# Another queue for one value chunk, and shorter fillers, in the prologue of a fused attention and feed-forward kernel

## The chip, the cores and the metric

The kernel runs on one core of a Trainium2 chip. A core has a matrix engine (TensorE, PE in the profile), a vector engine (VectorE, DVE), an activation engine (ScalarE, ACT), a general engine (GpSimd, POOL) and an engine that only issues transfers (SyncE, SP). Sixteen DMA engines carry all transfers, whichever engine issues them. Each engine runs its own instructions in their order, and semaphores order them against each other. The metric is the device time of one execution in microseconds; smaller is better.

## The reference

An attention layer with two parts is followed by a feed-forward layer. `q`, `k` and `v` are 8 batches x 8 heads x 576 positions x 64 numbers.

```python
q_d, k_d, v_d = (t.reshape(B, H, 144, 4, D).mean(axis=3) for t in (q, k, v))
out_up = np.repeat(softmax(scale * q_d @ k_d.T) @ v_d, 4, axis=2)
mask = np.abs(pos[:, None] - pos[None, :]) < 4          # a band of 7 keys per query
out_local = softmax(np.where(mask, scale * q @ k.T, -1e9)) @ v
x = (out_up + out_local).transpose(0, 2, 1, 3).reshape(4608, 512)
h = x @ w_in                                             # 512 -> 2048
out = (h * sigmoid(1.702 * h)) @ w_out                   # 2048 -> 512
```

All inputs and the output are fp32; the kernel multiplies in bf16.

## The kernel before

The 4608 rows of `x` fall into 9 groups of 512 for the feed-forward part, and the attention goes batch by batch (576 rows). The loop over groups `g` runs the two products of group `g` (`mm1`, L682, and `mm2`, L746) and puts batch `g + 1`'s attention in slots between their matmuls. The order on every engine is the order of the program text; nothing is planned or rearranged. The change edits the prologue alone, L789 to L878, which computes batch 0's attention by itself and starts group 0's first product.

**Value chunks.** The 576 keys of a batch are held as five overlapping chunks of 2 x 64 keys. Chunk `i` of `vb` has one half on partitions 0 to 63 and one on 64 to 127, each filled by a transfer of its own. `load_vb` (L219) issues the two transfers on POOL, which reads fp32 from memory and writes bf16 to `vb`. `load_v` (L203) issues on SyncE and writes fp32 to a tile `vf`; a cast (`prep_v`, L305) then makes `vb` of it. Before the change, batches 0 and 1 use `load_vb`; `load_v` is first used for batch 2. If `load_v` is given a `gate`, an engine writes one element of `vf` first, and the transfers on SyncE wait for that write, as they overwrite it.

**POOL's order at the start** is: four transfers of `kb` and `qb` (with `iota` instructions among them), ten of `vb` (two for each chunk), the first quarter of `w_in` (`load_w_in(0, 512)`), two additions for `qdT` (`pool_qk`, L297 and L301), the other three quarters of `w_in`, the next batch's `kb` and `qb`, and half of `w_out`. An issue on POOL waits for the landing of the transfer that POOL issued eight before it.

**TensorE's order in the prologue** is: fillers (`warm`, L637, products of the zero tiles `wz`, bf16, or `wf`, fp32, which nobody reads); local scores of the first four heads (L355, L367); fillers; local scores of the other four (which wait for `qT`, L267); downsampled scores (L379); a filler; the downsampled values from chunks 0 and 1 (`prep_vd_pe`, L336, `kc` = 0); fillers; those from chunks 1, 2 and 3 (`kc` = 1); local attention times values for two head pairs (`av_local0`, L511, chunks 0 to 4 in order); the downsampled values from chunks 3 and 4 (`kc` = 2); scores (L379); the downsampled attention (`av_down0`, L525 and L534); the third head pair; a filler (L863); the turned sums (`transp_sum`, L576 and L587); the fourth pair; and from 24.00 us on the first feed-forward matmuls (L682), first on `w_in`'s first quarter.

**ScalarE's order** there: the selection matrices `psel` (L173 to L178), `exp_local` for the first four heads and for the other four (L417, writes `es`), `exp_down` (L423, writes `ed`), and the copies of `prep_vd_pe` (L345, writes `vd`).

Of the kernel before, what the change touches and what calls it, by code (L numbers as in the profile page):

```python
# [19 lines left out]
def kernel(  # L20
# [9 lines left out]
    nc = tc.nc  # L30
# [38 lines left out]
    PM = [psum.tile([128, 512], FP32, name=f"pm{i}") for i in range(2)]  # L69
# [8 lines left out]
    def pm_tile():  # L78
        turn["m"] += 1
        return PM[turn["m"] % 2]  # L80

    wz = consts.tile([128, 512], BF16, name="wz")
    wf = consts.tile([128, 512], FP32, name="wf")
    off = consts.tile([128, 60], BF16, name="off")
    psel = consts.tile([128, 7, 64], BF16, name="psel")
# [27 lines left out]
    def fill():  # L113
        nc.vector.memset(wz, 0.0)
        nc.vector.memset(wf, 0.0)
        for t in kdT:
            nc.vector.memset(t[:, SD:160, :], 0.0)
        for t in vbs:
            nc.vector.memset(t[:, :, :, 64:65], 1.0)
        for t in vds:  # L120
            nc.vector.memset(t[:, :, :, 64:65], 4.0)
        for t in es:
            nc.vector.memset(t[:, :, 300:304], 1.0)
        for t in eds:
            nc.vector.memset(t[:, :, 432:480], 1.0)


    def make_off():
        nc.vector.tensor_tensor(out=dm, in0=dm, in1=dm, op=ALU.mult)
        nc.vector.tensor_single_scalar(out=dm, in_=dm, scalar=9.5, op=ALU.is_lt)  # L130
        nc.vector.tensor_scalar(
            out=off, in0=dm, scalar1=-1.0, scalar2=1e6, op0=ALU.add, op1=ALU.mult
        )
# [13 lines left out]
    def make_bias():  # L147
        nc.vector.memset(bias[:, 3:4], -3.0)
        nc.vector.tensor_copy(out=bias[:, 0:2], in_=rv)
        nc.vector.tensor_scalar(  # L150
            out=bias[:, 0:2], in0=bias[:, 0:2], scalar1=-1.0, scalar2=400.0,
            op0=ALU.add, op1=ALU.mult,
        )
# [17 lines left out]
    def end_psel():  # L171
        for m in range(7):
            nc.scalar.activation(  # L173
                out=dp[:, m], in_=di[:, 0:64], func=AF.Abs, scale=8.0, bias=db[:, m : m + 1]
            )
        nc.scalar.activation(out=dp, in_=dp, func=AF.Relu, bias=bias[:, 3:4])
        for sl, c in ((slice(0, 1), 1), (slice(1, 7), 0)):
            nc.scalar.activation(  # L178
                out=psel[:, sl], in_=dp[:, sl],
                func=AF.Exp, scale=-400.0, bias=bias[:, c : c + 1],  # L180
            )
# [21 lines left out]
    def load_v(b, gate=None, chunks=range(5)):  # L203
        t = ldp.tile([128, 5, H, D], FP32, name="vf", tag="vf")
        vf[b] = t
        if gate is not None:
            gate(t[0:1, 0, 0, 0:1])
        for i in chunks:
            for par in range(2):
                nc.sync.dma_start(  # L210
                    out=t[64 * par : 64 * par + 64, i],
                    in_=bass.AP(
                        tensor=v.tensor,
                        offset=v[b, 0].offset + (114 * i + KSTART[par]) * D,
                        ap=[[D, 64], [S * D, H], [1, D]],
                    ),
                )

    def load_vb(b, i):  # L219
        for par in range(2):  # L220
            nc.gpsimd.dma_start(  # L221
                out=vbs[b % 2][64 * par : 64 * par + 64, i, :, 0:D],
                in_=bass.AP(
                    tensor=v.tensor,
                    offset=v[b, 0].offset + (114 * i + KSTART[par]) * D,
                    ap=[[D, 64], [S * D, H], [1, D]],
                ),
            )
# [34 lines left out]
    def prep_1(name, b, qd):  # L263
        store, dst = {"k": (kf, kT), "q": (qf, qT)}[name]
        tt = work.tile([128, S, 2], BF16, name=f"{name}T{qd}", tag=f"{name}T{qd}", bufs=1)
        t32 = tt.rearrange("p t a -> p (t a)").bitcast(FP32)
        nc.vector.transpose(  # L267
            out=t32.rearrange("p (i c) -> p c i", c=18),
            in_=store[b, qd].bitcast(FP32).rearrange("p (c d) -> p c d", c=18),
        )  # L270
        dst[b, qd] = tt
# [33 lines left out]
    def prep_v(b, eng, i=slice(0, 5), h=slice(0, H)):  # L305
        cp = eng.copy if eng is nc.scalar else eng.tensor_copy
        cp(out=vbs[b % 2][:, i, h, 0:D], in_=vf[b][:, i, h])  # L307
# [17 lines left out]
    def prep_vd_pe(b, pv, kcs=range(3), between=None):  # L325
        hp0, n = 0, HP
        vb, vd = vbs[b % 2], vds[b % 2]
        for kc, iis in ((0, (0, 1)), (1, (1, 2, 3)), (2, (3, 4))):
            if kc not in kcs:
                continue  # L330
            c0 = 256 * (kc - kcs[0])
            if between and kc == 1:
                between()
            for i in iis:
                for j in range(2):
                    nc.tensor.matmul(  # L336
                        pv[64 * j : 64 * j + 64, c0 : c0 + D * n],
                        lhsT=psel[:, PSEL.index((i, kc)), :],
                        rhs=vb[:, i, :, :].rearrange(
                            "p (hp j) d -> p hp j d", j=2  # L340
                        )[:, hp0 : hp0 + n, j, 0:D],
                        start=(i == iis[0]), stop=(i == iis[-1]),
                        tile_position=(0, 64 * j),
                    )
        nc.scalar.copy(  # L345
            out=vd[:, kcs[0] : kcs[-1] + 1, :, 0:D],
            in_=pv[:, 0 : 256 * len(kcs)].rearrange(
                "p (k h d) -> p k h d", k=len(kcs), h=HP
            ),
        )  # L350
# [26 lines left out]
    def score_d(b, qd, sd, kc, a, r):  # L377
        rows, j = slice(32 * r, 32 * r + 32), r % 2
        nc.tensor.matmul(  # L379
            sd[64 * j : 64 * j + 64, r // 2, SD * kc : SD * kc + SD],  # L380
            lhsT=kdT[qd][rows, 48 * kc : 48 * kc + 64, a],
            rhs=qdT[b, qd][rows, :, a],
            start=(a == 0), stop=(a == 1),
            tile_position=(32 * r, 64 * j),
        )

    def scores(b, qd, sp):
        bar_others(sp)
        for i in range(5):
            for a in range(2):  # L390
                for par in range(2):
                    for r in range(4):
                        score(b, qd, sp, i, a, par, r, barred=True)
        return sp

    def scores_d(b, qd, sd):
        for kc in range(3):
            for a in range(2):
                for r in range(4):
                    score_d(b, qd, sd, kc, a, r)  # L400
        return sd
# [13 lines left out]
    def exp_local(qd, sp):  # L415
        for u in range(2):
            nc.scalar.activation(  # L417
                out=es[2 * qd + u][:, :, 0:300], in_=sp[u][:, :, 0:300],
                func=AF.Exp, scale=inv_sqrt_d,
            )  # L420

    def exp_down(qd, sd):
        nc.scalar.activation(  # L423
            out=eds[qd][:, :, 0:432], in_=sd[:, :, 0:432],
            func=AF.Exp, scale=inv_sqrt_d / 16.0,
        )
# [115 lines left out]
    def y_tiles0():  # L542
        return (
            work.tile([128, 2, 6, D], BF16, name="yl", tag="yl", bufs=4),
            work.tile([128, 2, 2, D], BF16, name="yd", tag="yd", bufs=4),
            work.tile([128, 2, 7, 1], FP32, name="rc0", tag="rc0", bufs=4),
        )
# [89 lines left out]
    def warm(n, cols=512, t=None, z=wz):  # L637
        t = pm_tile() if t is None else t
        for _ in range(n):
            nc.tensor.matmul(  # L640
                t[:, 0:cols], lhsT=z[:, 0:128], rhs=z[:, 0:cols], start=True, stop=True
            )
# [150 lines left out]
    load_1("q", q, qf, 0, 1)  # L793
    iota_psel()
    fill()
    for i in range(5):
        load_vb(0, i)
    load_w_in(0, 512)
    warm(3, z=wf)
    warm(2)  # L800
    make_off()
    make_ident(di)
    make_psel()
    make_bias()
    end_psel()
    prep_1("k", 0, 0)
    prep_1("q", 0, 0)
    sp = scores(0, 0, PA[0:2])
# [13 lines left out]
    warm(2, z=wf)  # L822
    sp = scores(0, 1, PA[0:2])
    exp_local(1, sp)
    exp_down(0, scores_d(0, 0, PA[2]))
    for hp in range(4):
        o[hp] = PA[hp % 3]
        y[hp] = y_tiles0()
    warm(1, z=wf)
    prep_vd_pe(0, PM[0], range(0, 2), lambda: warm(2, t=PM[1]))  # L830
    for hp in range(2):
        av_local0(hp, o[hp], range(5))
        normalise0(o[hp], y[hp], hp % 2, "a")
# [18 lines left out]
    def av_whole0(hp):  # L852
        av_local0(hp, o[hp], range(5))
        av_down0(hp, o[hp])
        normalise0(o[hp], y[hp], hp % 2)
# [4 lines left out]
        copy_x(0, hp, PM if n is None else PA[n][:, :, 0:288])  # L860

    av_whole0(2)
    warm(1, t=PM[0], z=wf)  # L863
    turned(0, None)
    av_whole0(3)
    turned(1, 1)
# [90 lines left out]
```

## Time and profile before

| what | value |
|---|---|
| median of three runs | 316.63 us (315.98 to 320.5) |
| profiled execution: time, span of the instructions | 317.56 us, 315.8 us |
| TensorE busy | 307.7 us, 97% of the span |
| first feed-forward matmul (L682) starts | 24.00 us |
| idle time of TensorE just before 16.66 us, 22.56 us, 24.89 us | 0.24, 1.11, 0.29 us |
| granted TensorE clock, mean | 0.998 |
| landing of chunks 3 and 4 of `vb`, second halves | 15.69 us, 16.62 us |
| landing of the first quarter of `w_in` | 20.7 us |

Times within the kernel count from the span's start. A line of a timeline gives start and duration in microseconds, the engine, the line of the kernel, the operation, what it writes and reads, shape and type, and how many; in brackets stands the idle time of the engine before it and what ended it, where "issue" means that the engine waited for nothing that the profile shows. A line of the view by windows gives the stretch, its length, then for TensorE's matmuls, its weight loads, VectorE, ScalarE and GpSimd the busy time with the number of instructions started, and then the granted clock, the DMA share and GB/s. In the DMA view q0 is POOL's queue, q1 SyncE's, and q8 carries instructions; a line gives packets, MB and the time that the packets took as a share of 16 engines. A landing is the time from issue until the last of a transfer has arrived.

### The profile page before, as it was taken

The page shows a single profiled execution, that of the slowest core. Times are in us where ns is not written, and L with a number is a line of the kernel's source. Part 1 is how long each engine was busy: PE and PEld are TensorE (multiplying, and loading weights), DVE is VectorE, ACT ScalarE, POOL GpSimd, SP SyncE. Part 2 cuts the span into 40 slices and gives each one's busy share as a digit, 9 for nine tenths or more (in the row PEclk, how much of TensorE's full clock was granted, in tenths as well). Part 3 has the DMA queues.
Part 4 walks back from the last instruction along what each step waited for, and adds up shares of the span by engine and source line. Part 5 has one row for each costly group of instructions (what it writes and reads, how often), then busy time and mean ns, then how long its engine had stood idle before and what let it go on. Part 6 is the DMA issues. An engine that isn't in the chain of part 4 may idle for free.

```text
span 315.8 us, 10270 instructions
## 1 busy us (share of the span) xinstructions
PE 307.7 (97%) x4543; PEld 154.3 (49%) x4543; DVE 123.5 (39%) x247; ACT 190.2 (60%) x348; POOL 138.8 (44%) x170
## 2 busy tenths in 40 slices
PE   7989999999999999999999999999999999999995
PEld 3455455445544455455544554455445544444444
DVE  6763824720673057604760377027801640000000
ACT  5445882767657685668566856584767576316611
POOL 8863782179339920794079505960393000000000
PEclk9999999999999999999999999999999999999999
DMA  7999999999959913995299519971920110020011
GB/s 119 122 187 210 187 86 205 190 196 261 181 162 224 202 47 98 188 204 113 87 203 206 112 56 206 208 136 39 173 46 11 58 71 2 15 85 33 2 66 66
DMA packets 64075, 39.97 MB, mean 127 GB/s; under 512 B 44064, under 2 KB 55456, under 8 KB 64032
## 3 DMA queue, kind: packets, MB, share of 16 engines
q1 hardware_dynamic: 44496, 24.32, 36.0%
q0 software_dynamic: 19392, 14.95, 33.5%
q8 instruction: 35, 0.57, 0.8%
q14 instruction: 8, 0.07, 0.1%
q10 hardware_dynamic: 144, 0.07, 0.1%
HBM read 44.83 MB, written 9.44 MB: 172 GB/s over the span
## 4 chain that ended last, share of the span: by engine, by line
PE 91%; DMA 4%; ACT 1%; POOL 1%; issue 1%; DVE 0%; POOLq 0%; DVEq 0%; ACTq 0%
PE pm L746 36%; PE pm L682 35%; PE pa L682 4%; PE pa L367 2%; PE pa L439 2%; DMA qb<-in_q_dram 2%; PE pa L490 2%; PE pa L379 2%; PE pa L746 2%; PE pa L448 2%; DMA vb<-in_v_dram 1%; PE pm L761 1%; ACT od L610 1%; PE pm L640 0%; POOL vb L221 0%
## 5 line engine op out<-in xcount | busy, mean ns | idle before, releaser
L746 PE MATMUL pm<-w_out_bf,gT 128*128 128x512 bf16 x528 | 120.3, 380 | 0.0
L682 PE MATMUL pm<-xT,w_in_bf 128*128 128x512 bf16 x512 | 119.2, 379 | 0.5 <-ACT xT L603 0.3
L693 ACT ACTIVATE gT<-pm 128x512 bf16<-128x512 f32 x128 | 76.3, 598 | 43.7 <-PE pm L682 43.7
L682 PEld LDWEIGHTS <-w_in_bf 128*128 128x128 bf16 x576 | 55.7, 98 | 66.9 <-issue 1.1
L746 PEld LDWEIGHTS <-gT 128*128 128x128 bf16 x560 | 52.3, 98 | 60.7 <-issue 0.5
L431 DVE TENSOR_TENSOR es<-es,mask 128x600 bf16<-128x600 bf16 x28 | 19.0, 694 | 97.0 <-ACT es L417 96.3
L297 POOL TENSOR_TENSOR pq<-kT 128x576 f32<-128x576 bf16 x13 | 15.1, 1165 | 60.8 <-DVE kT L267 60.8
L731 ACT ACTIVATE osb<-pm 128x512 f32<-128x512 f32 (+2 forms) x35 | 20.4, 587 | 25.8 <-PE pm L746 23.0
L476 DVE TENSOR_TENSOR y<-pa,rc 128x896 bf16<-128x896 f32 x28 | 30.6, 1092 | 1.0
L480 ACT COPY y<-y 64x64 bf16<-64x64 bf16 x28 | 6.7, 241 | 31.3 <-DVE y L476 31.3
L417 ACT ACTIVATE es<-pa 128x600 bf16<-128x600 f32 x32 | 19.7, 668 | 8.7 <-PE pa L367 8.6
L313 POOL TENSOR_TENSOR v<-v 112x512 f32<-112x512 f32 x18 | 23.0, 1279 | 0.0
L307 POOL CAST vb<-vf 128x2560 bf16<-128x2560 f32 x6 | 13.9, 2318 | 19.8 <-DMA out_dram<-osb 6.3
L267 DVE STREAM_TRANSPOSE kT<-kb 128x576 f32<-128x576 f32 x16 | 19.9, 1246 | 5.8 <-DMA kb<-in_k_dram 5.6
L733 DVE TENSOR_SCALAR osb<-pm 128x128 f32<-128x128 f32 x1 | 0.3, 292 | 55.2 <-ACT osb L731 55.2
L632 DVE TENSOR_TENSOR xT<-pa,od 128x456 bf16<-128x456 bf16 (+2 forms) x84 | 16.6, 255 | 12.3 <-ACT od L610 12.1
L267 DVE STREAM_TRANSPOSE qT<-qb 128x576 f32<-128x576 f32 x16 | 19.9, 1243 | 0.8 <-DMA qb<-in_q_dram 0.4
L682 PE MATMUL pa<-xT,w_in_bf 128*128 128x512 bf16 x64 | 20.0, 379 | 0.0
L610 ACT COPY od<-pa 128x256 bf16<-128x256 bf16 (+1 forms) x56 | 18.3, 410 | 1.1 <-PE pa L490 0.4
L367 PEld LDWEIGHTS <-kT 32*64 32x64 bf16 x1280 | 14.2, 104 | 6.9 <-issue 4.1
L221 POOL DMA_DIRECT2D vb<-in_v_dram x20 | 13.7, 703 | 8.6 <-DMA w_in_bf<-in_moe_w_in_dram 3.6
L367 PE MATMUL pa<-qT,kT 32*64 32x60 bf16 x1280 | 16.5, 198 | 0.5 <-DVE qT L267 0.5
(90 smaller groups left out, 275.9 us busy)
## 6 DMA issues: line engine op xcount, KB each, us to landing
out_dram<-osb SPq DMA_DIRECT2D x35, 256.0 KB, 2.4
vf<-in_v_dram SPq DMA_DIRECT2D x60, 128.0 KB, 6.8
v<-in_v_dram SPq DMA_DIRECT2D x36, 192.0 KB, 5.4
kb<-in_k_dram POOLq DMA_DIRECT2D x16, 288.0 KB, 7.7
qb<-in_q_dram POOLq DMA_DIRECT2D x16, 288.0 KB, 8.9
w_in_bf<-in_moe_w_in_dram POOLq DMA_DIRECT2D x4, 512.0 KB, 9.2
w_out_bf<-in_moe_w_out_dram POOLq DMA_DIRECT2D x4, 512.0 KB, 12.5
vb<-in_v_dram POOLq DMA_DIRECT2D x20, 64.0 KB, 5.9
```

The source lines that it names most:

```text
L267: nc.vector.transpose(out=t32.rearrange("p (i c) -> p c i", c=18), in_=store[b, qd].bitcast(FP32).rearrange("p (c d) -> p c d", c=18),)
L313: eng.tensor_tensor(out=t1[0:112], in0=x[:, :, 0:2, :], in1=x[:, :, 2:4, :], op=ALU.add)
L367: nc.tensor.matmul(sp[r // 2][64 * par : 64 * par + 64, r % 2, 60 * i : 60 * i + 60], lhsT=kT[b, qd][rows, k0 : k0 + 64, a], rhs=qT[b, qd] ...
L417: nc.scalar.activation(out=es[2 * qd + u][:, :, 0:300], in_=sp[u][:, :, 0:300], func=AF.Exp, scale=inv_sqrt_d,)
L431: nc.vector.tensor_tensor(out=ev, in0=ev, in1=mask, op=ALU.mult)
L476: nc.vector.tensor_tensor(out=y.rearrange("p (x c) d -> p x c d", x=2), in0=ov[:, :, :, 0:D], in1=rc.to_broadcast([128, 2, 7, D]), op=ALU. ...
L610: nc.scalar.copy(out=od[:, 4 * t0 : 4 * (t0 + n)].rearrange("p (t f) -> p t f", f=4), in_=x[:, xx, c0 : c0 + n, None].to_broadcast([128, n ...
L632: nc.vector.tensor_tensor(out=sub(xT[hp], t0 + at, *dims), in0=sub(x, col, *from_x), in1=sub(od, at, *dims), op=ALU.add,)
L682: nc.tensor.matmul(acc, lhsT=w_in_bf[:, dmc, ffc * 128 : (ffc + 1) * 128], rhs=xT[dmc][:, g * TG : g * TG + TG], start=(dmc == 0), stop=(d ...
L693: nc.scalar.activation(out=gT[:, ffc, :], in_=acc, func=AF.Silu, scale=GELU_SCALE)
L731: eng.activation(out=osb, in_=ap, func=AF.Copy, scale=1.0 / GELU_SCALE)
L746: nc.tensor.matmul(ops[t], lhsT=gT[:, ffc, t * 128 : (t + 1) * 128], rhs=w_out_bf[:, ffc, :], start=(ffc == 0), stop=(ffc == n_ffc - 1),)
```

## The change

Chunk 4 of batch 0's values is no longer loaded by POOL (`range(4)` for `range(5)`). Instead `load_v` loads it as fp32 on SyncE's queue into `vf`, behind a gate: ScalarE copies one element of `psel` into the chunk, just after it has made `psel`. The gate's element now lies in the first chunk that is loaded, which is the same place as before for the other uses. ScalarE casts the chunk to `vb` between `exp_local(1, ...)` and `exp_down(0, ...)`. `w_in` and everything behind it on POOL are issued two transfers sooner. Four places of fillers on TensorE are changed: 2 x 512 columns to 2 x 256 (first scores); one fp32 product of 512 columns to two bf16 of 128 (before chunk 0's use); 2 x 512 to 2 x 256 (between `kc` = 0 and 1); and one fp32 product of 512 to two bf16 of 512 (before the turned sums).

```diff
@@ load_v
         if gate is not None:
-            gate(t[0:1, 0, 0, 0:1])
+            gate(t[0:1, chunks[0], 0, 0:1])
@@ prologue
     fill()
-    for i in range(5):
+    for i in range(4):
         load_vb(0, i)
     load_w_in(0, 512)
     warm(3, z=wf)
-    warm(2)
+    warm(2, 256)
     make_off()
     make_ident(di)
     make_psel()
     make_bias()
     end_psel()
+    load_v(0, lambda t: nc.scalar.copy(out=t, in_=psel[0:1, 6, 0:1]), [4])
     prep_1("k", 0, 0)
...
     sp = scores(0, 1, PA[0:2])
     exp_local(1, sp)
+    prep_v(0, nc.scalar, 4)
     exp_down(0, scores_d(0, 0, PA[2]))
...
-    warm(1, z=wf)
-    prep_vd_pe(0, PM[0], range(0, 2), lambda: warm(2, t=PM[1]))
+    warm(2, 128)
+    prep_vd_pe(0, PM[0], range(0, 2), lambda: warm(2, 256, t=PM[1]))
...
     av_whole0(2)
-    warm(1, t=PM[0], z=wf)
+    warm(2, t=PM[0])
     turned(0, None)
```

## The prediction

> **What bounds the kernel now.** I read the page's first two parts, then TensorE's timeline of the first 25 us, then the DMA view. TensorE is the bound: busy 97% of the span, and from 24.00 us on it stands still for hardly a microsecond before the tail. The change edits only the prologue, so what it is worth is by how much it moves the first matmuls of the dense part (L682, 24.00 us).
>
> ```profile
> PE 307.7 (97%) x4543; PEld 154.3 (49%) x4543; DVE 123.5 (39%) x247; ACT 190.2 (60%) x348; POOL 138.8 (44%) x170
> ...
> q8 instruction: 35, 0.57, 0.8%
> ```
>
> TensorE's timeline (start, duration, engine, line):
>
> ```profile
> 13.68 1.12 PE L640 MATMUL pm<-wf 128*128 128x512 f32 x2
> 14.74 0.42 PE L336 MATMUL pm<-vb,psel 128*64 128x256 bf16 x4
> 15.09 0.60 PE L640 MATMUL pm<-wz 128*128 128x512 bf16 x2
> 15.62 0.53 PE L336 MATMUL pm<-vb,psel 128*64 128x256 bf16 x6
> 16.09 0.34 PE L511 MATMUL pa<-vb,es 64*64 64x65 bf16 x17
> 16.66 0.41 PE L511 MATMUL pa<-vb,es 64*64 64x65 bf16 x23 [0.24 <-DMA vb<-in_v_dram]
> ...
> 19.94 1.12 PE L640 MATMUL pm<-wf 128*128 128x512 f32 x2
> ...
> 22.56 0.33 PE L587 MATMUL pm<-id,yl 128*128 128x57 bf16 x5 [1.11 <-issue]
> ```
>
> Two waits stand there. The 0.24 us at 16.66 is the one that the change removes: chunk 4 lands at 16.62. The other, 1.11 us at 22.56, waits for no engine and no data ("issue"). It comes from instruction loading. 35 packets of 16 KB on q8 for 9086 matmuls and weight loads are one per 260 instructions (63 bytes each), so I take blocks of 256 of 64 bytes. The view by windows counts what had started before the wait at 22.56, before the one other "issue" wait in the attention (53.57) and before 16.13:
>
> ```profile
> 0.00:16.13 16.13, 13.62 (x222) 6.44 (x225) 11.35 (x32) 7.84 (x16) 13.49 (x30) 1.00 1.38 121
> 0.00:21.60 21.60, 18.64 (x351) 9.52 (x351) 15.77 (x45) 10.97 (x20) 18.14 (x37) 1.00 1.33 137
> 0.00:53.50 53.50, 49.05 (x862) 25.46 (x863) 29.86 (x62) 30.65 (x53) 35.86 (x60) 1.00 1.32 158
> ```
>
> TensorE stands after 702 and after 1725 instructions: 1023 apart, four blocks. So a block ends at 702, and the one before it at about 447, reached at 16.13 in the first L511 matmuls. I read it so: passing 447 asks for the block that begins at 703. The DMA view narrowed to 20.0 to 20.5 us holds that block's packet:
>
> ```profile
> q8 instruction: 1, 0.02, 11.2%
> ```
>
> It starts at 20.11, takes 0.9, and TensorE goes on at 22.55: **6.42 us from the request to use**. This is the chain that sets 22.55; the 1.06 us filler at 20.01 lies inside it. What decides is when L511 begins, and before it L336 needs chunk 3. The second half of chunk 3 is issued at 10.99 and lands 4.7 later, at 15.69:
>
> ```profile
> DMA to landing us min/median/max: 4.7/4.7/4.7
> ```
>
> The L336 matmuls on chunk 3 start at 15.77, 0.08 later. **Chunk 3, not chunk 4, sets the request.**
>
> **The change part by part.** *Fillers.* The first wz pair (0.84 at 7.01) falls to half: 0.2 us at most, since L367 waits for qT (8.06); the next scores wait for qT at 12.04 anyway. Then 1.06 us of fp32 becomes two of 128 columns (0.1), and 0.43 becomes 0.22: TensorE would reach chunk 3's matmuls 1.2 us sooner and now waits there for the landing instead. The last fp32 filler becomes two bf16 ones, 1.06 to 0.43: 0.63 less, ahead of the block wait. Each filler keeps its number of matmuls and loads (the fp32 one is recorded as two of each), so block ends stay at the same instructions.
>
> *POOL.* Two issues of 0.69 go, so w_in's first piece is issued at 11.7, not 12.99, qdT's sums end at 14.4, not 15.76 (used at 17.36), and the pieces behind follow 1.4 sooner. Worth nothing: w_in's first piece lands at 20.7 and is first used at 24.00.
>
> *ScalarE.* The gate copy (0 to 0.24, the 64x64 copy of L480) follows psel at 8.29, in an idle stretch until 9.19. The cast is taken as 0.59 (L345's cast of 128x512), behind es at 14.15. It waits for the landing: SyncE's queue is empty until 52.71, its two issues go out at about 8.5 and 9.2, and vf transfers land after 6.8 us (median of 60), so 16.0; the bounds are 1.6 (the quickest store), so no wait, and 17. Behind the cast stand exp_down (0.90) and vd's copy; with 16.0 the first ends at 17.5 and the second finds its matmuls done at about 17. av_down0 (17.99 now) asks for them at about 19. Cover: 1.5 us here, and 1.7 us in the block wait (below). Nothing on the path.
>
> *The DMA engines.* Here is the cost. Chunk 4's 1024 packets leave the end of POOL's queue, where they delayed nobody but themselves, and go out on SyncE's queue while chunks 0 to 3 are in flight. Packets by queue in 10:11, 99:100, 102:103 and 76:78 us:
>
> ```profile
> q0 software_dynamic: 1206, 0.15, 248.8%
> ```
> ```profile
> q1 hardware_dynamic: 987, 0.26, 131.0%
> ```
> ```profile
> q0 software_dynamic: 101, 0.21, 113.2%
> ```
> ```profile
> q0 software_dynamic: 173, 0.35, 91.5%
> q1 hardware_dynamic: 173, 0.04, 16.2%
> ```
>
> With both queues full they go packet for packet (173 and 173). A 256-byte packet of q1 costs one of 16 engines 16.2 ns alone (16/987 us). Beside q0 it costs more: a pair takes 2 us x 16/173 = 185 ns, q0's alone 16/101 = 158, so 27. SyncE's 64 packets per engine, begun near 10 us, are through long before chunk 3's end, and all of them stand ahead of it: 64 x 16.2 = 1.0 to 64 x 27 = 1.7 us; zero is the other bound, if an engine overlaps the two queues. I take 1.1, near the row of the same packet alone: chunk 3 at 16.8, its matmuls at 16.9, the request at 17.2 instead of 16.13.
>
> *The block wait.* The following requests in a full queue (22.55, 53.57) have packets at 26.23 and 57.16: 3.7 and 3.6 us, where this one took 3.97. [...] I take 3.9, so 0.1 off. TensorE needed 21.45 - 16.13 = 5.3 us from the request to the block's end, now 4.7 without the fillers, against 6.3: the wait grows from 1.11 to about 1.6 and swallows the 0.63.
>
> Sum: +1.1 - 0.1 = **+1.0 us** on the start of the dense part, and TensorE's work behind it is unchanged. The profiled execution took 317.56 us (span 315.8, 1.8 around it), the median of the three runs is 316.63. So 318.6 against 317.56, or 317.6 against the median.
>
> **The rivals.** *On time (0.22):* SyncE's packets cost POOL's nothing, or wait behind them. Chunk 3 lands at 15.7, the request stays at 16.13, and a late chunk 4 is covered as above: 316.6 +- 0.3. For it: after the issue at 52.71 no q1 packet runs until past 56 while q0 is full. Against: the 173 and 173.
>
> *A gain (0.12):* the block's packet starts sooner. With a delay of 2.6, the lowest that I found in a full queue (48.6 to 51.2), it gives 1.3 back; with chunk 3 half as late (0.5) that is 315.8. More than 1.7 sooner is worth nothing, as TensorE arrives by then.
>
> *The block is no bound (0.05):* the 1.11 us were a chance. Then chunk 3's 1.1 later, less 0.63 of filler and the 1.11: -0.6, 316.0. [...]
>
> *Slow clock (0.06):* the trimmed fillers leave TensorE still for 1 to 1.3 us twice before 16.9 (for chunks 2 and 3) and for 1.6 before 23. The granted clock reads 1.00 throughout, yet wz matmuls lie 0.43 apart at 7.01 and w_in's 0.22, after some 6 us of work. Dropping back for 6 us doubles TensorE's work, less the 1.6 of cover: +2 to +3 on top, 320. No wait of up to 1.11 us has slowed matmuls behind it, so it decides only beyond that. [...]
>
> **The numbers.** Forecast 0.55, and 0.22, 0.12, 0.05, 0.06. The range goes from the gain (315.8) to SyncE's dearest packet and the same delay (+1.7 + 0.4 for runs that differ by 0.3%) with a little of the clock's case: 319.0. A measurement of this kernel tells about 2% (6.3 us) from no change; every case lies inside: 0.01 faster, 0.97 the same, 0.02 slower.
>
> **What would show it.** Right: chunk 3's second half lands near 16.8, L336 then waits for the DMA of vb, the "issue" wait before L587 is 1.5 to 1.8, the instruction after 702 starts 6.2 to 6.4 us after the 447th, and L682 starts near 25. Wrong: a landing at or before 15.7, a 447th instruction before 16.1, no wait before L587, or matmuls 0.43 apart.

## The result, and the profile after

| | before | after |
|---|---|---|
| median (lowest to highest) | 316.54 us (315.87 to 320.5) | 320.69 us (318.07 to 322.26) |
| profiled execution: time, span | 317.56, 315.8 us | 319.48, 317.7 us |
| granted TensorE clock, mean of that execution | 0.998 | 0.989 |
| chunk 3's second half lands | 15.69 us | 17.80 us |
| first feed-forward matmul (L682) starts | 24.00 us | 26.32 us |
| from there to the end of the span | 291.8 us | 291.4 us |

Each median is over 18 runs; they lie 4.15 us apart. The ratio is 1.0112, with a 95% interval of 1.0094 to 1.013: the changed kernel is 1.1% slower, which is below the 2% from which a difference counts here. The forecast was +1.0 us and the range ended at 319.0. The last row places the loss in the two profiled executions, which lie 1.9 us apart: all of it lies ahead of 26.32 us. Most runs of after lose more than this one.

Three lines of the page of after (busy time by engine, TensorE's clock in 40 slices of 7.9 us, the instruction queue):

```profile
PE 307.2 (97%) x4543; PEld 155.1 (49%) x4543; DVE 122.2 (38%) x247; ACT 191.0 (60%) x350; POOL 137.2 (43%) x168
...
PEclk9968999999999999999999999999999999999999
...
q8 instruction: 35, 0.57, 0.8%
```

As many TensorE instructions as before and as many instruction packets; but the clock falls in the third and fourth slices. TensorE's timeline of after (start, duration, engine, line) shows what stands ahead of the fall, and what follows it:

```profile
13.69 0.28 PE L640 MATMUL pm<-wz 128*128 128x128 bf16 x2
13.90 0.42 PE L336 MATMUL pm<-vb,psel 128*64 128x256 bf16 x4
14.25 0.39 PE L640 MATMUL pm<-wz 128*128 128x256 bf16 x2
14.58 0.42 PE L336 MATMUL pm<-vb,psel 128*64 128x256 bf16 x4
17.84 0.30 PE L336 MATMUL pm<-vb,psel 128*64 128x256 bf16 x2 [2.85 <-DMA vb<-in_v_dram]
18.08 0.57 PE L511 MATMUL pa<-vb,es 64*64 64x65 bf16 x40
18.57 0.55 PE L336 MATMUL pm<-vb,psel 128*64 128x256 bf16 x4
19.05 0.93 PE L379 MATMUL pa<-qdT,kdT 32*64 32x144 bf16 x24
...
24.24 0.70 PE L587 MATMUL pm<-id,yl 128*128 128x114 bf16 x8
...
26.32 0.59 PE L682 MATMUL pm<-xT,w_in_bf 128*128 128x512 bf16 x2
```

Chunks 0, 1 and 2 are used and done by 15.0; then TensorE stands still for 2.85 us until chunk 3 lands. From 18.57 on the same instructions take longer: the 24 matmuls of L379 take 0.93 us, where the kernels at full clock below show 0.58. The wait before L587 is gone. The view by windows gives the clock (stretch, length, five engines, granted clock, DMA share, GB/s):

```profile
16.00:17.00 1.00, 0.00 (x0) 0.00 (x0) 0.00 (x0) 0.00 (x0) 1.00 (x2) 1.00 1.35 198
17.00:18.00 1.00, 0.16 (x2) 0.11 (x2) 0.00 (x0) 0.78 (x2) 1.00 (x3) 1.00 1.27 213
18.00:19.00 1.00, 1.00 (x46) 0.59 (x44) 0.39 (x2) 1.00 (x2) 0.75 (x2) 0.86 1.23 202
19.00:20.00 1.00, 1.00 (x28) 0.76 (x28) 0.97 (x3) 0.48 (x2) 0.15 (x1) 0.50 1.23 203
...
25.00:26.00 1.00, 1.00 (x34) 0.74 (x33) 0.12 (x1) 0.43 (x2) 0.56 (x1) 0.73 1.19 224
26.00:27.00 1.00, 0.91 (x13) 0.52 (x12) 0.97 (x3) 0.48 (x1) 0.00 (x0) 1.00 1.12 205
```

The clock stays at 1.00 during the wait, drops to 0.50 at about 18.7 (0.86 over the microsecond from 18), 0.9 us after TensorE has gone on, and comes back at about 25.5 (0.73 over the one from 25). That is some 6.8 us at half speed. All 18 runs of after have lost clock: 10 show a mean of 0.982 to 0.984, 7 of 0.988 or 0.989, one of 0.995. (The 0.998 of before is no such loss: its clock drops in the last 1.1 us of the span, when TensorE has no matmul left.) The missing clock of 0.984, 0.989 and 0.995, times a span of 318 us, over 0.5, is the time at half speed: 10.2, 7.0 and 3.2 us, steps of some 3.4. The medians follow it: 320.77, 320.23, and 318.07 for the one run.

### The profile page after: what moved, and what is told of

It is laid out like the page before. It is cut to its first block, busy times and chain, and to the rows that moved or that the text cites. A ratio compares the mean times of both kernels' runs of the same rounds, so it can differ in the third digit from the quotient of the medians.

```text
span 317.7 us, 10276 instructions
## 1 busy us (share of the span) xinstructions
PE 307.2 (97%) x4543; PEld 155.1 (49%) x4543; DVE 122.2 (38%) x247; ACT 191.0 (60%) x350; POOL 137.2 (43%) x168
## 4 chain that ended last, share of the span: by engine, by line
PE 92%; DMA 4%; ACT 1%; POOL 1%; issue 1%; DVE 0%; POOLq 0%; ACTq 0%
PE pm L746 36%; PE pm L682 35%; PE pa L682 4%; PE pa L367 2%; PE pa L379 2%; PE pa L439 2%; DMA qb<-in_q_dram 2%; DMA vb<-in_v_dram 2%; PE pa L490 2%; PE pa L746 2%; PE pa L448 2%; PE pm L761 1%; ACT od L610 1%; PE pm L640 0%; PE pa L525 0%
## 5 line engine op out<-in xcount | busy, mean ns | idle before, releaser
L682 PE MATMUL pm<-xT,w_in_bf 128*128 128x512 bf16 x512 | 119.2, 379 | 0.5 <-ACT xT L603 0.3
L682 PEld LDWEIGHTS <-w_in_bf 128*128 128x128 bf16 x576 | 55.6, 98 | 66.9 <-issue 1.1
L431 DVE TENSOR_TENSOR es<-es,mask 128x600 bf16<-128x600 bf16 x28 | 17.1, 624 | 101.2 <-ACT es L417 100.4
L682 PE MATMUL pa<-xT,w_in_bf 128*128 128x512 bf16 x64 | 20.0, 379 | 0.0
L307 POOL CAST vb<-vf 128x2560 bf16<-128x2560 f32 x6 | 13.9, 2319 | 13.9 <-DMA vf<-in_v_dram 11.6
L297 POOL TENSOR_TENSOR pq<-qT 128x576 f32<-128x576 bf16 x14 | 16.0, 1145 | 0.1
```

Of the source, the lines that this page charges most:

```text
L297: nc.gpsimd.tensor_tensor(out=t1, in0=sv[:, :, 0:2, :], in1=sv[:, :, 2:4, :], op=ALU.add)
L431: nc.vector.tensor_tensor(out=ev, in0=ev, in1=mask, op=ALU.mult)
L682: nc.tensor.matmul(acc, lhsT=w_in_bf[:, dmc, ffc * 128 : (ffc + 1) * 128], rhs=xT[dmc][:, g * TG : g * TG + TG], start=(dmc == 0), stop=(d ...
```

## The experiments

The theories at the start: **clock** (the wait halves TensorE's clock, and that alone is the loss), **landing** (the late chunk 3 itself costs the time), **blocks** (the instruction block's fetch follows the late matmuls, as predicted), and **fillers** (shorter fillers alone let the clock fall). Each ratio is to the kernel before, run on the same chip, with its 95% interval.

### One half of the change at a time

`e1_load_only` has the changed loads, with all fillers as before:

```diff
 # against the changed kernel
-    warm(2, 256)
+    warm(2)
...
-    warm(2, 128)
-    prep_vd_pe(0, PM[0], range(0, 2), lambda: warm(2, 256, t=PM[1]))
+    warm(1, z=wf)
+    prep_vd_pe(0, PM[0], range(0, 2), lambda: warm(2, t=PM[1]))
...
-    warm(2, t=PM[0])
+    warm(1, t=PM[0], z=wf)
```

> Chunk 4 by SyncE and ScalarE's cast as in the change, the fillers as before. All theories: chunk 3 lands at 17.8 us as in the changed kernel, since the transfers are the same. TensorE reaches its matmuls at 15.8, so it waits 2.0 us instead of 2.85. Slow clock (the wait behind short fillers lets the granted clock fall to 0.50, and that is most of the loss): with more work before the wait the clock stays at 1.00 or falls for a shorter time; no block wait, first feed-forward matmul at 24.0 - 1.1 + 2.0 = 24.9 us, 317.5 us. Late landing (the 2.1 us of chunk 3 are the loss, the clock is a side effect): 319 us or more, whatever the clock. Fillers (the short fillers alone do it): 316.5 us.

Measured: 1.0115 (1.0036 to 1.0193). Its four runs fall into two pairs: 318.26 and 317.77 us at a clock of 1.0, 321.45 and 321.58 at 0.989 and 0.988. So the loads alone can bring the clock down, and **the fall costs 3.5 us here** (321.5 - 318.0). The profiled execution is one at full clock; its timeline has

```profile
18.19 0.30 PE L336 MATMUL pm<-vb,psel 128*64 128x256 bf16 x2 [1.70 <-DMA vb<-in_v_dram]
...
19.27 0.58 PE L379 MATMUL pa<-qdT,kdT 32*64 32x144 bf16 x24
...
24.63 0.38 PE L682 MATMUL pm<-xT,w_in_bf 128*128 128x512 bf16 x1
```

Chunk 3 is used 2.4 us later than before (15.77), yet L682 starts only 0.63 later. So most of the lateness is made up, but not all: the two runs at full clock still lie 1.4 us over the median of the kernel before (316.61).

`e2_fillers_only` has the loads of before and the four changed filler places:

```diff
 # against the kernel before
-    warm(2)
+    warm(2, 256)
...
-    warm(1, z=wf)
-    prep_vd_pe(0, PM[0], range(0, 2), lambda: warm(2, t=PM[1]))
+    warm(2, 128)
+    prep_vd_pe(0, PM[0], range(0, 2), lambda: warm(2, 256, t=PM[1]))
...
-    warm(1, t=PM[0], z=wf)
+    warm(2, t=PM[0])
```

> Chunk 4 by POOL as before, with the changed kernel's shorter fillers. All theories: chunk 3 lands at 15.7 us. TensorE waits about 1 us for it. Fillers: the clock falls to 0.50 and the time is 319 to 321 us. Slow clock: a wait of 1 us is too short, the clock stays at 1.00. Then, if the request for the next block of instructions leaves sooner because TensorE's sequencer gets past it sooner (as the changed kernel suggests, where the packet starts at 17.5 and no wait is left), the block wait of 1.11 goes too: first feed-forward matmul at 24.0 - 1.1 - 0.6 = 22.3, 314.9 us. If the block wait of the prediction holds (6.4 us from the first local product at 16.1), it grows to 1.7 and the time stays at 316.5.

Measured: 1.003 (0.9999 to 1.0061), 317.67 us. In 5 of 10 runs the clock is 0.998 or higher (316.17 to 318.05), in the others lower: 318.51 to 319.58 at 0.984 to 0.989, and one of 316.19 at 0.994. In the profiled execution, at full clock, TensorE waits for chunks 2 and 3:

```profile
15.43 0.30 PE L336 MATMUL pm<-vb,psel 128*64 128x256 bf16 x2 [0.52 <-DMA vb<-in_v_dram]
16.66 0.31 PE L336 MATMUL pm<-vb,psel 128*64 128x256 bf16 x2 [0.93 <-DMA vb<-in_v_dram]
```

So **short fillers alone trip the clock about every second time**, with waits that in this execution are well under those of after. Each half of the change can bring the fall by itself; together they brought it in every run.

### Filling the wait

`e3_busy_wait` is the changed kernel with 13 fillers of 512 columns between the matmuls on chunk 2 and those on chunk 3 (26 TensorE instructions more):

```diff
-    def prep_vd_pe(b, pv, kcs=range(3), between=None):
+    def prep_vd_pe(b, pv, kcs=range(3), between=None, before_3=None):
...
+                if before_3 and (kc, i) == (1, 3):
+                    before_3()
...
-    prep_vd_pe(0, PM[0], range(0, 2), lambda: warm(2, 256, t=PM[1]))
+    prep_vd_pe(0, PM[0], range(0, 2), lambda: warm(2, 256, t=PM[1]),
+               lambda: warm(13, t=PM[1]))
```

> The changed kernel with 13 more fillers (bf16, 512 columns, 0.216 us each, 2.8 us) between the uses of chunk 2 and chunk 3, so that TensorE works while it waits for chunk 3. Slow clock: chunk 3 still lands at 17.8, the clock stays at 1.00, the work from 17.84 to the first feed-forward matmul takes 6.3 us instead of 8.5: 24.1 us, and the time is 316 to 317 us, 3.5 to 4 below the changed kernel. Late landing: as the changed kernel, 320 to 321. Fillers (those that were shortened): also 320 to 321, since they stay short elsewhere.

Measured: 318.0 us, 1.0044 (1.0026 to 1.0061), and a clock of 1.0 in all ten runs. From its timeline (line numbers are 2 higher here; the traces of the experiments miss the records of some matmuls, as of one of these 13, and a gap of 0.16 us stands where one is missing):

```profile
15.31 2.75 PE L642 MATMUL pm<-wz 128*128 128x512 bf16 x12 [0.16 <-issue]
17.99 0.30 PE L338 MATMUL pm<-vb,psel 128*64 128x256 bf16 x2
...
83.86 0.25 PE L450 MATMUL pa<-vd,ed 48*64 48x65 bf16 x3 [0.60 <-issue]
```

Chunk 3 is as late as in after, its first feed-forward matmul starts at 23.92, no later than before, and the clock's loss is gone. That left 1.4 us over the kernel before, with an "issue" wait at 83.86 that the kernel before does not have. `e9` and `e10` part these.

`e9_same_count` fills the same wait without one instruction more than the changed kernel has: fp32 fillers, which are recorded as two matmuls each, take the place of the short bf16 ones, and the last filler goes:

```diff
-    warm(2, 128)
-    prep_vd_pe(0, PM[0], range(0, 2), lambda: warm(2, 256, t=PM[1]))
+    warm(1, z=wf)
+    prep_vd_pe(0, PM[0], range(0, 2), lambda: warm(2, t=PM[1], z=wf))
...
-    warm(2, t=PM[0])
```

> The changed kernel, kept busy while it waits for chunk 3, at an unchanged number of instructions: one fp32 product of 512 columns for the two of 128, two fp32 products for the two of 256, and the last two bf16 fillers are gone. Chunk 3 lands near 17.9, TensorE waits for it 0.3 to 0.5 us, the clock stays at 1.00, every block of instructions from 703 on begins where it did. If the loss of the run with 13 more fillers (1.4 us) was the late landing: 317.5 to 318.2 us. If it was mainly its blocks, moved by 26 instructions (it shows a wait of 0.60 at one of them, 83.9 us): 316.3 to 317.2.

Measured: 316.97 us, **1.0001 (0.9985 to 1.0017)**, the clock 0.998 or higher in all 12 runs. Its timeline:

```profile
15.52 1.98 PE L640 MATMUL pm<-wf 128*128 128x512 f32 x4
17.43 0.42 PE L336 MATMUL pm<-vb,psel 128*64 128x256 bf16 x4
18.25 0.31 PE L336 MATMUL pm<-vb,psel 128*64 128x256 bf16 x2 [0.41 <-DMA vb<-in_v_dram]
...
22.19 0.45 PE L587 MATMUL pm<-id,yl 128*128 128x114 bf16 x8
...
23.75 0.38 PE L682 MATMUL pm<-xT,w_in_bf 128*128 128x512 bf16 x1
```

Chunk 3 lands at 18.21 here, 2.5 us later than in the profile of before, and L682 starts at 23.75, 0.25 sooner. From the use of chunk 3 to L682 the kernel before took 8.2 us, this one 5.5: the wait before L587 (1.11), the last filler (1.06) and the wait for chunk 4 (0.24) are not there, and 0.3 of smaller things. After keeps two bf16 fillers (0.43) where this kernel has no last filler. With that, an estimate from these lines for after at full clock is 17.84 + 5.5 + 0.43 = 23.8 for the start of L682, against 24.00 before and the 26.32 measured. So the **landing theory falls**: with the trimmed fillers the late chunk would have cost about nothing, and the loss of after is the clock's. With the fillers of before it is not free: `e1` at full clock starts L682 0.63 later, as much as the trim of the last filler saves.

### How little stillness is enough

`e4_half_packets` sends half of the packets on SyncE's queue. It loads and casts only 4 of the 8 heads of chunk 4; the other heads' part of that chunk is zeros, so this part of the attention is left out:

```diff
-    def load_v(b, gate=None, chunks=range(5)):
+    def load_v(b, gate=None, chunks=range(5), heads=H):
...
+    nc.vector.memset(vbs[0][:, 4, 4:8, 0:D], 0.0)
...
-    load_v(0, lambda t: nc.scalar.copy(out=t, in_=psel[0:1, 6, 0:1]), [4])
+    load_v(0, lambda t: nc.scalar.copy(out=t, in_=psel[0:1, 6, 0:1]), [4], heads=4)
...
-    prep_v(0, nc.scalar, 4)
+    prep_v(0, nc.scalar, 4, slice(0, 4))
```

> The changed kernel with half of chunk 4's transfer: SyncE loads and ScalarE casts four of its eight heads, and the other four are zeros, so this part of the attention is left out. Every theory takes the landing of chunk 3 to go with the packets ahead of it: 15.7 + 2.1 / 2 = 16.75 us (the prediction's 17 to 27 ns for a packet would give 16.2 to 16.55). TensorE's wait shrinks from 2.85 to 1.8 us. Slow clock: at 1.8 us the clock falls seldom or not at all, 316.5 us; if it falls as in the changed kernel, 319 to 320. Late landing: half of the loss, 318.6. Fillers: 320 to 321.

Measured: 320.5 us, 1.0111 (1.0073 to 1.015), a clock of 0.984 to 0.989 in all four runs. Chunk 3 landed at 16.89. Timeline, and the same execution by windows:

```profile
15.37 0.30 PE L336 MATMUL pm<-vb,psel 128*64 128x256 bf16 x2 [0.68 <-DMA vb<-in_v_dram]
...
16.93 0.43 PE L336 MATMUL pm<-vb,psel 128*64 128x256 bf16 x2 [1.26 <-DMA vb<-in_v_dram]
```
```profile
16.00:17.00 1.00, 0.07 (x2) 0.07 (x2) 0.00 (x0) 0.43 (x2) 1.00 (x3) 0.50 1.20 192
```

Two waits of 0.68 and 1.26 us with a little work between are as dear as one of 2.85, and the clock is already at 0.50 in the second of them: it fell at about 15.9, when 0.3 us of that wait had passed. It stayed down until 26.2, for 10.2 us, yet L682 starts at 26.31, no later than in the profile of after with its 6.8 us: in part of this half speed TensorE stood still anyway. So the loss follows neither the length of the longest wait nor the time at half speed alone.

### Moving the packets

`e5_early` issues SyncE's two transfers ahead of everything, without a gate, so that they do not meet chunk 3:

```diff
+    load_v(0, None, [4])
     load_qk(0, 0)
...
-    load_v(0, lambda t: nc.scalar.copy(out=t, in_=psel[0:1, 6, 0:1]), [4])
```

> The changed kernel with chunk 4's two SyncE transfers issued first of all, without the gate, so that their packets run ahead of or beside q and k instead of beside chunks 0 to 3. If what counts is that 64 packets per engine stand ahead of chunk 3 (2.1 us, 33 ns each), all but what runs before POOL's first packets at 2.4 us is still there: q and k land up to 1.5 us later, chunk 3 at 16.5 to 17.3, and the clock falls in most runs: 318.5 to 320.5 us. If only the mixing of the two queues' small packets is dear, chunk 3 lands near 15.9 and the time is 316 to 317.5.

Measured: 316.46 us, 0.9983 (0.9959 to 1.0007). Chunk 3 lands at 16.82 and L682 starts at 23.96, but the packets now stand ahead of `qb`, and TensorE waits there:

```profile
9.91 0.83 PE L367 MATMUL pa<-qT,kT 32*64 32x60 bf16 x80 [3.12 <-DVE qT L267]
```

This profile shows a clock of 0.50 from 11.6 to 15.0 us, and 4 of the 10 runs have a mean of 0.989 to 0.994. `e11_early_busy` keeps these loads, puts the fillers around `prep_vd_pe` back as they were before, and makes the first pair one fp32 filler, to hold the clock:

```diff
 # against e5_early
-    warm(2, 256)
+    warm(1, z=wf)
...
-    warm(2, 128)
-    prep_vd_pe(0, PM[0], range(0, 2), lambda: warm(2, 256, t=PM[1]))
+    warm(1, z=wf)
+    prep_vd_pe(0, PM[0], range(0, 2), lambda: warm(2, t=PM[1]))
```

> Chunk 4's transfers first of all on SyncE (as in the early run), with the fillers of before, and the first pair of bf16 fillers replaced by one fp32 product (the same four instructions, some 0.6 us longer), so that TensorE is busier while it waits for q. Slow clock: it falls in fewer runs than in the early run (5 of 10 below 1.00), the wait of 0.24 for chunk 4 is gone, chunk 3 at 16.3 to 16.9 is as late as in most executions of before: 315.8 to 316.6 us, no better than the early run's undisturbed ones. If the later q and k decide instead: 317 to 318.

Measured: 316.83 us, 1.0007 (0.999 to 1.0024), the clock below 0.998 in one run of 12. Chunk 3 lands at 16.37. The clock is held, yet nothing is gained over the kernel before. It is held although this execution, too, has a long wait for `qT`, longer than any in `e4`:

```profile
10.39 0.83 PE L367 MATMUL pa<-qT,kT 32*64 32x60 bf16 x80 [2.29 <-DVE qT L267]
```

So the length of a single wait does not tell whether the clock falls.

### The instruction blocks

The prediction's chain rested on blocks of 256 instructions. `e6_small_fillers` is the kernel before with the fp32 filler ahead of chunk 0 replaced by 28 bf16 fillers of 64 columns, 52 instructions more:

```diff
-    warm(1, z=wf)
+    warm(28, 64)
     prep_vd_pe(0, PM[0], range(0, 2), lambda: warm(2, t=PM[1]))
```

> The kernel before, its fp32 filler of 1.06 us ahead of chunk 0's use replaced by 28 bf16 products of 64 columns, about as long, but 56 instructions instead of 4. If the 1.11 us before 22.56 are the loading of a block of 256 instructions, the ends of all blocks move 52 instructions forward: the request leaves within these fillers, near 14.4 us instead of 16.1, the wait before L587 goes, and a wait of 0 to 1.4 us stands 52 instructions earlier, in the third head pair's products (19.4): 315.5 to 316.8 us. If the 1.11 us were something of L587 itself, they stay where they are: 316.6.

Measured: 319.36 us, 1.0071 (1.0045 to 1.0098). The waits have moved, and the counts by windows say where to:

```profile
14.91 0.42 PE L640 MATMUL pm<-wz 128*128 128x64 bf16 x9 [0.49 <-issue]
...
20.39 0.22 PE L511 MATMUL pa<-vb,es 64*64 64x65 bf16 x4 [0.43 <-issue]
```
```profile
0.00:14.60 14.60, 11.86 (x223) 6.20 (x224) 11.34 (x32) 7.50 (x16) 12.05 (x28) 1.00 1.64 125
0.00:20.20 20.20, 16.37 (x349) 9.08 (x351) 14.07 (x41) 10.67 (x20) 17.50 (x36) 1.00 1.54 137
```

TensorE stands after 447 instructions, and again after 700 recorded ones (351 loads, and two matmuls fewer, whose records are missing), though other matmuls stand at those places now. **The ends of blocks at 447 and 702 are thereby shown**; the wait before L587 is gone. The first feed-forward matmul starts at 23.68, so the loss comes later, and a longer wait stands there:

```profile
84.43 0.35 PE L448 MATMUL pa<-vd,ed 48*64 48x65 bf16 x16 [1.53 <-issue]
```

Not all of the loss is this. Three of its 11 runs have a clock of 0.988 to 0.995; in the other eight the median is 318.85 us, 1.9 over the kernel before. And the time less the span, 1.73 to 1.85 us in every run of the kernel before, is up to 2.5 here and up to 2.9 in `e7`; why is not shown. `e7_small_and_trim` adds the trimmed last filler to that:

```diff
 # against e6_small_fillers
-    warm(1, t=PM[0], z=wf)
+    warm(2, t=PM[0])
```

> As the run with 28 small fillers, and the last fp32 filler (1.06 us, ahead of the turned sums) becomes two bf16 products (0.43). If the block's end no longer lies behind that filler, its 0.63 us come off in full: first feed-forward matmul at 22.3 to 23.4, 314.9 to 316.2 us, the clock at 1.00. If a wait moves in instead, no gain against the run without the trim.

Measured: 318.87 us, 1.0055 (1.0033 to 1.0078); the wait at the block's end, 0.43 in `e6`, is 1.53 here:

```profile
21.22 0.27 PE L511 MATMUL pa<-vb,es 64*64 64x65 bf16 x4 [1.53 <-issue]
...
23.35 0.70 PE L587 MATMUL pm<-id,yl 128*128 128x114 bf16 x8
```

The second line shows what follows: the eight matmuls take 0.70 us, as in after, where `e9` has 0.45. The granted clock of this execution is 0.50 from 21.1 to 24.5, and 7 of the 12 runs have a mean of 0.989 to 0.995. So a wait for instructions, too, was followed by a fall of the clock, with no late data in it.

`e8_last_filler` has only this trim, in the kernel before:

```diff
 # against the kernel before
-    warm(1, t=PM[0], z=wf)
+    warm(2, t=PM[0])
```

> The kernel before with only its last fp32 filler (1.06 us) turned into two bf16 products (0.43). The prediction said that the block wait behind it swallows what it saves: the wait before L587 grows from 1.11 to 1.7 and the time stays at 316.6. If the block is no bound: 0.63 less, 316.0, with the wait as it was.

Measured: 316.67 us, 0.9989 (0.9968 to 1.0009), which is -1.0 to +0.3 us: no gain is shown, but one of 0.63 us is not excluded either. The wait before L587 did not grow in the profiled execution; it read 0.33 us, where the profile of before has 1.11 (and `e2`, with the same trim, 0.83):

```profile
21.49 0.33 PE L587 MATMUL pm<-id,yl 128*128 128x57 bf16 x5 [0.33 <-issue]
```

So this wait differs by up to 0.8 us between these profiles, and a single profile does not give its size. `e10_shift_26` adds 13 fillers of 16 columns to the kernel before, as many instructions as `e3` had:

```diff
-    prep_vd_pe(0, PM[0], range(0, 2), lambda: warm(2, t=PM[1]))
+    prep_vd_pe(0, PM[0], range(0, 2), lambda: [warm(2, t=PM[1]), warm(13, 16, t=PM[1])])
```

> The kernel before with 13 more fillers of only 16 columns (26 instructions, some 0.3 us, ahead of chunk 3's use, where it waits anyway in most executions), and nothing else. It measures what 26 more instructions cost by moving the ends of all blocks. If moved blocks explain the 1.4 us of the run with 13 more fillers: 317.5 to 318.2 us, with a wait for issue in an attention stage of a later batch (near 84 us). If not: 316.5 to 317.1.

Measured: 318.88 us, 1.0059 (1.0031 to 1.0087). Two of its waits by line:

```profile
PE pa L448 <- issue: 0.9, 1, 0.9
...
PE pa L534 <- issue: 0.6, 1, 0.6
```

26 instructions more, with next to no work in them, cost 0.6%. Three of its 10 runs have a clock of 0.993 to 0.995 and take 319.6 to 320.8 us; the other seven have a median of 317.71, which is 0.9 us over the kernel before. `e3` was left with 1.4 us at a clock of 1.0, and `e9`, with as late a chunk and no instruction more than after, with none. So moved block ends are the likely cause of what `e3` was left with; how much of the 1.4 us they are is not settled by these runs.

### The landing of chunk 3, over all runs

The tile view of the profiles gives one landing of chunk 3's second half for each. In after, issued at 10.99, it landed 6.8 us later:

```profile
DMA to landing us min/median/max: 6.8/6.8/6.8
```

Without SyncE's packets beside it: 15.69 (before), 16.62, 16.21, 15.79, 16.18, 15.97 (`e2`, `e6`, `e7`, `e8`, `e10`), mean 16.08. With them: 17.80 (after), 18.14, 17.82, 18.21 (`e1`, `e3`, `e9`), mean 17.99. But POOL issues this half only once a part of `qb` has landed, at 10.6 to 11.4 us, and the landings vary with that too. From issue to landing it takes 4.6 to 5.6 us without them (mean 5.1) and 6.7 to 7.2 with them (mean 6.9). So 64 packets per engine delay it by 1.8 us, 28 ns each. With 32 (`e4`) it takes 6.1 (it lands at 16.89), that is 1.0 us or 31 ns each.

`w_in`, which is issued sooner and so closer behind chunk 3, is a rival for this delay. `e5` and `e11` speak against it: there `w_in` follows chunk 3 by 0.7 us as well, without SyncE's packets beside it, and chunk 3 takes 4.6 and 3.2 us.

## Why the prediction was wrong

**The place and the bound: right.** The change acts in the prologue alone (291.8 and 291.4 us from L682 to the end).

**Chunk 3, not chunk 4: right.** SyncE's packets go ahead of chunk 3, and TensorE waits there for `vb` at L336. But the term was mis-sized. Against the 1.1 us that I took (17 ns a packet), the runs show 1.8 (28 ns), at the end of the range that I had from the row at 76 us (27). The landing that I added it to, 15.69, was moreover the earliest of the six. Both put chunk 3 at 17.8 instead of 16.8, and TensorE, which had run through chunks 0 to 2 without a pause, stood still once for 2.85 us instead of twice for 1 to 1.3.

**The block wait follows the late request: wrong.** This step was to carry chunk 3's delay to L682. After has no wait before L587, which was one of the prediction's own signs of being wrong; nor have `e1`, `e3` and `e9`. The DMA view of after, narrowed to 17.4 to 17.6 us, holds the block's packet, which starts at 17.49, and the view by windows shows what TensorE had started by then:

```profile
q8 instruction: 1, 0.02, 35.1%
```
```profile
0.00:17.49 17.49, 11.12 (x216) 5.99 (x216) 11.35 (x32) 7.51 (x17) 14.87 (x32) 1.00 1.31 145
```

432 instructions, where I had the request wait for the 447th. It left while TensorE stood before chunk 3, so it does not wait for that instruction to run; what lets it leave, no run here shows. Nor does one show the 0.1 that I took off for a delay of 3.9 us from that instruction to the packet: in after the packet came first. The blocks were right (`e6`: 447 and 700); whether the wait swallows the trimmed filler, `e8` leaves open. But a delay of chunk 3 does not push the block; it takes the place of the block wait. Without the fall of the clock the start of L682 would have been about unchanged (23.8 by the estimate from `e9`, against 24.00). The forecast of +1.0 was wrong in its chain, not only in its size.

**ScalarE's cast: right in effect.** `vf`'s second transfer landed at 17.12, later than the 16.0 that I took and than the bound of 17, and the cast ran at 17.22 in 0.62 us. `e9`, with this cast in its place, loses nothing.

**The slow clock: the step that failed the forecast.** I gave this rival 0.06 and only "a little" of the range, on the sentence that it "decides only beyond" 1.11 us. I took the longest gap that had done no harm for a safe one, although the rival itself had gaps beyond it. It then happened in 18 runs of 18. That its price (320) lies near the result is partly luck: it was 317.6 plus 2 to 3 us, where the chain's +1.0 in it did not come true and the fall cost more. In the order of TensorE's stillness before chunk 3's matmuls, taken from the one profile of each kernel (lost clock: a mean below 0.998):

| kernel | waits for chunks 2 and 3 | runs with lost clock |
|---|---|---|
| before, beside the experiments | none | 1 of 80 |
| `e9_same_count` | 0.41 | 0 of 12 |
| `e2_fillers_only` | 0.52 and 0.93 | 5 of 10 |
| `e1_load_only` | 1.70 | 2 of 4 |
| `e4_half_packets` | 0.68 and 1.26 | 4 of 4 |
| after | 2.85 | 18 of 18 |

The table is no rule: `e11` waited 2.29 us for `qT` and lost clock in 1 run of 12.

What a fall costs: after's seven runs at 0.988 to 0.989 have a median of 320.23 us, 3.3 over `e9`, and 7.0 us at half speed leave 3.5 us of work undone. `e2`'s two runs at 0.989 (318.5) lie only 1.9 over the median of its runs at full clock (316.68). The ten runs of after with a further 3.2 us at half speed have a median only 0.5 higher, where 1.6 us of work is undone. `e4`'s profile, with as long a half speed, shows one way to that: a part of it falls on a wait.

**What stays open.** Which share of stillness, over which stretch, brings the clock down was not measured; the waits vary between executions, and each kernel has one profile. Four profiles hold a stretch at half speed ahead of the end, and it lasts 3.4 us (`e5`, `e7`), 6.8 (after) and 10.2 (`e4`). In the 3.4 us just before the fall TensorE was busy for some 0.9 us (after), 1.7 (`e5`, `e7`) and 2.2 (`e4`). In `e11` the wait of 2.29 us reaches from 8.10 to 10.39, so the 3.4 us from 8.10 to 11.50 hold no more than 1.1 us of work, and the clock of that execution is 1.0. As that is less than in `e5`, `e7` and `e4`, the busy time of such a stretch alone is not the measure either.

## What to carry to other kernels

Fillers ahead of a late transfer are not only there to pass the time: as long as the data comes late they hold the clock (1.0 in all ten runs of `e3`, 0.998 or higher in all twelve of `e9`), so trim them only by what the landing has really moved, and read the landing from several executions. A transfer taken off one queue and put on another can go ahead of what was in flight and still needed first (here it put chunk 3 back by 1.8 us); name the transfer that lands last before and after. When fillers are compared, keep TensorE's instruction count the same, or the ends of its instruction blocks move and bring waits of their own (0.4 to 1.5 us in `e6`, `e7` and `e10`).

## What the runs showed of the hardware

- The granted clock fell to 0.50 within the second of two waits of 0.68 and 1.26 us with two matmuls between (`e4`), 0.9 us after the end of a wait of 2.85 (after) and at the end of a wait of 1.53 for instructions (`e7`); it did not fall behind one of 2.29 (`e11`). The time at half speed comes in steps of some 3.4 us, and two of them cost 3.3 to 3.5 us (after, `e1`), in `e2` 1.9.
- 26 instructions of almost no work cost 0.6% (`e10`) and 52 cost 0.7% (`e6`). Their profiles show waits of 0.4 to 1.5 us at ends of instruction blocks that fall on other matmuls, and in some runs the clock fell as well.
- A 256-byte packet of SyncE's queue delayed POOL's transfer by 28 to 31 ns on each DMA engine, where the same packet took 16.2 alone.
